# Three weight conversions shared with GpSimd and started a unit earlier, output rows in buffers of their own, and another end of the last block

## The chip, the cores and the metric

The kernel runs on one core of a Trainium2 chip. The core has five engines that run side by side and each take their own instructions strictly in order: PE (TensorE, matmuls and transposes), DVE (VectorE), ACT (ScalarE), POOL (GpSimd) and SP (SyncE, which here only issues DMAs). The metric is the device time of one execution in microseconds (us), the median of several runs.

## What is computed

The input is `q`, `k`, `v`, `alpha` of shape (4, 8, 768, 48) in float32 and two weight matrices in float64. A gated linear attention runs over the 768 positions, and its output goes through a feed-forward network (FFN) of 2048 hidden columns:

```python
for t in range(S):
    state = alpha[:, :, t, :, None] * state + np.einsum('bhd,bhe->bhde', k[:, :, t], v[:, :, t])
    y[:, :, t] = np.einsum('bhd,bhde->bhe', q[:, :, t], state)
x = np.ascontiguousarray(y.transpose(0, 2, 1, 3)).reshape(B * S, H * D)   # 3072 x 384
h = x @ w_in                                                              # 384 x 2048
g = np.maximum(0.01 * h, h)
out = g @ w_out                                                           # 2048 x 384
```

## The kernel before, in words

**Units and blocks.** The attention is cut into 24 units of 128 positions of one batch (4 batches at each of 6 places). Three units make a block of 384 rows, the FFN's moving size; there are 8 blocks. The FFN runs over 16 slices f of 128 hidden columns. `ffn_in(i, f)` is 9 matmuls (three groups of rows, each high*high, high*low and low*high part), then two passes on ACT and two on DVE that make `gh` and `gl`. `ffn_out(i, f)` is 9 matmuls into three PSUM banks, one for each unit of the block, summed over f. `finish(i)` copies the three banks out and stores them.

**The front.** Blocks 0 and 1 run interleaved over f, since the weights come in meanwhile: (0, f), (1, f). Before that, units 0 to 8 (`AHEAD` = 9) run through the attention alone; then PE has FFN work without a break. A unit's steps are: scans of alpha (`scans`, lines L283 to L298 with `pc`, `rc` on DVE and two small copies on POOL), `qs` and `ks` (L313, L321), scores on PE (L330), a copy on ACT and a triangular mask on POOL (L340, L341), the outputs `y` on PE (L368, L374), ACT's and DVE's halves of `y` into the tile `large` (L391, L392), and the new state (`us` L406 on DVE, a product on POOL L346). When a block's three units are done, `gather` sends two DMAs from `large` to `large` (L416); the FFN of that block waits for them.

**Conversions.** A slice's weights land in `raw` by five DMAs of SP: `w_out` (L192) and four pieces of `w_in` (L188), 786 KB together. `converting(f)` makes from each float64 a high and a low float32: on ACT a scaling of the top words (L224) and the rounded high part (L232); on DVE `bits` (L226, L229), the power `pw` (L236), the rest of the value (L238), the low words by their power (L240) and the sum (L243). The first three (f = 0, 1, 2, `EARLY`) run in the front, each placed behind the `ks` of unit 6, 7 and 8; the others run in the stage of blocks 0 and 1. The table `LOADS` says behind which DMA of the front the loads of the first four slices are issued.

**The order of the work.** The program is written step by step with generators; a scheduler then places each instruction on its engine, and `behind(key)` forbids it to place one ahead of a named instruction. What stands on an engine runs in that order whatever comes late. Buffers of a name (`t`, `o`, banks `a` and `b`) are handed out again when their last reader is done.

Of the kernel before, what the change touches and what calls it, by code (L numbers as in the profile page):

```python
# [9 lines left out]
F32 = mybir.dt.float32  # L10
# [12 lines left out]
def gated_linear_attn_ffn(ctx, tc, q, k, v, alpha, w_in, w_out, out):  # L23
    nc = tc.nc
# [180 lines left out]
    def converting(f, ordered=False):  # L205
# [31 lines left out]
        yield  # L237
        put(ordered, "DVE", lambda: nc.vector.tensor_tensor(val, val, hi.bitcast(F32), ALU.subtract))  # L238
# [5 lines left out]

    def convert(f):
        for _ in converting(f):
            pass
# [227 lines left out]
    pos = {}  # L475

    def ffn_out(i, f, gs, tag):
        gh, gl = gs
        if f == 0:
            pos[i] = [bank(tag)[:, 0:DM] for _ in range(UPB)]  # L480
        po = pos[i]
        for j in range(UPB):
            js = slice(j * C, (j + 1) * C)
            for n, (gt, wn) in enumerate(((gh, HIGH), (gh, LOW), (gl, HIGH))):
                nc.tensor.matmul(  # L485
                    po[j], gt[:, js], w_out_of(f, wn), start=f == 0 and n == 0, stop=f == NF - 1 and n == 2
                )
        if f == NF - 1:
            finish(i)

    def finish(i):
        for j, po in enumerate(pos.pop(i)):
            tb, b = units[i * UPB + j]
            o = ffp.tile([P, DM], F32, name="t")
            nc.scalar.copy(o, po)  # L495
            r = b * S + tb * C
            nc.sync.dma_start(out[r:r + P, :], o)
# [10 lines left out]
    LOADS = [(("v", 4), 0, 0), (("v", 5), 0, 1), (("v", 6), 1, 0), (("v", 7), 1, 1), (("g", 1), 2, None), (("g", 1), 3, None)]  # L508
# [3 lines left out]
    loaded_f = converted = 0  # L512
    for n, _ in enumerate(st):
        if n == 2:
            load_values(NV - 1)
        while LOADS and LOADS[0][0] in made:
            key, f, part = LOADS.pop(0)
            with behind(*key):
                load_weights(f, part)
            loaded_f = f + 1  # L520
        u = AHEAD - EARLY + converted
        if converted < EARLY and ("ks", u) in made:
            with behind("ks", u):
                convert(converted)
            converted += 1
        if n in STARTS:
            i, f = items[len(gs)][:2]
            with behind(*STARTS[n]):
                gs[len(gs)] = ffn_in(i, f)
# [175 lines left out]
```

## Time and profile before

| | |
|---|---|
| median of 3 runs | 541.69 us (540.21 to 541.97) |
| the profiled execution | 540.7 us |
| its span, first to last instruction | 539.0 us |
| PE busy | 520.6 us (97% of the span) |
| PE weight loads busy | 497.8 us (92%) |
| DVE busy | 380.3 us (71%) |
| ACT busy | 234.1 us (43%) |
| POOL busy | 64.5 us (12%) |
| granted TensorE clock, mean | 0.996 of full speed |

The share of an engine is a mean over stages that differ: the front (0 to about 71 us), blocks 0 and 1 (to about 167 us), and blocks 2 to 7 with the attention of units 9 to 23 between their matmuls. The profiled execution took 1.7 us more than its span, and 1.0 us less than the median of the runs.

### The profile page before, as it was taken

How to read it: one execution, taken by the hardware profiler on the slowest of the kernel's cores; microseconds unless marked ns; L12 is line 12 of the kernel's file. 1: busy time of each engine (PE TensorE's matmuls, PEld its weight loads, DVE VectorE, ACT ScalarE, POOL GpSimd, SP SyncE). 2: the span in 40 equal slices, each digit the busy share in tenths (PEclk: the TensorE clock that was granted, in tenths of full speed). 3: DMA queues.
4: the chain of work that ended last, by engine and by line, in shares of the span. 5: the costliest groups of instructions: out<-in, count | busy, mean ns of one | idle time of the engine just before them, and what ended most of it. 6: DMA issues, size and time to landing. Idle time of an engine off the chain costs nothing.

```text
span 539.0 us, 9954 instructions
## 1 busy us (share of the span) xinstructions
PE 520.6 (97%) x3742; PEld 497.8 (92%) x3742; DVE 380.3 (71%) x694; ACT 234.1 (43%) x494; POOL 64.5 (12%) x140
## 2 busy tenths in 40 slices
PE   6998899999999899999999999999999999999996
PEld 4787789999998799999999999999999999999995
DVE  6899999999999597875685775775876533333331
ACT  2675665545532543435334343344343344233332
POOL 4445420000000022110110101001100000000000
PEclk9998999999999999999999999999999999999999
DMA  9999954545825343433332422413301010101001
GB/s 146 164 177 184 202 140 131 142 111 134 190 43 144 114 107 85 102 79 103 71 82 58 105 64 61 105 42 99 69 1 40 0 45 1 23 0 45 0 1 49
DMA packets 92981, 46.62 MB, mean 86 GB/s; under 512 B 57856, under 2 KB 90112, under 8 KB 92928
## 3 DMA queue, kind: packets, MB, share of 16 engines
q1 hardware_dynamic: 92928, 45.93, 39.4%
q8 instruction: 31, 0.51, 0.4%
q14 instruction: 22, 0.18, 0.1%
HBM read 38.83 MB, written 4.72 MB: 81 GB/s over the span
## 4 chain that ended last, share of the span: by engine, by line
PE 87%; DVE 5%; DMA 3%; issue 1%; SPq 1%; POOL 1%; ACT 1%; DVEq 0%; ACTq 0%; POOLq 0%
PE ph L460 35%; PE b L485 32%; PE a L330 4%; PE a L485 4%; PE a L374 3%; PE a L368 2%; PE b L258 2%; PE a L353 1%; DMA raw<-in_moe_w_in_dram 1%; DMA out_dram<-t 1%; PE a L385 1%; DVE pc L288 1%; PE b L374 1%; PE a L258 1%; DVE rc L294 1%
## 5 line engine op out<-in xcount | busy, mean ns | idle before, releaser
L460 PE MATMUL ph<-large,w 128*128 128x384 f32 x1152 | 225.6, 338 | 3.1 <-DMA raw<-in_moe_w_in_dram 1.9
L460 PEld LDWEIGHTS ph<-large,w 128*128 128x128 f32 x1152 | 200.5, 188 | 5.4 <-DVE t L466 2.2
L485 PE MATMUL b<-w,gh 128*128 128x384 f32 x672 | 169.6, 340 | 1.3 <-ACT t L495 1.3
L466 DVE TENSOR_TENSOR t<-ph,t 128x384 f32<-128x384 f32 x128 | 70.3, 549 | 86.7 <-ACT t L463 86.3
L485 PEld LDWEIGHTS b<-w,gh 128*128 128x128 f32 x672 | 119.5, 188 | 3.7 <-ACT t L495 1.6
L463 ACT ACTIVATE t<-ph 128x384 f32<-128x384 f32 x128 | 62.6, 489 | 136.7 <-PE ph L460 128.6
L468 ACT CAST gh<-t 128x384 fp32r<-128x384 f32 x128 | 65.7, 513 | 108.2 <-DVE t L466 104.7
L485 PE MATMUL b<-w,gl 128*128 128x384 f32 x336 | 107.3, 336 | 0.0
L472 DVE TENSOR_TENSOR gl<-t,gh 128x384 fp32r<-128x384 f32 x128 | 70.3, 550 | 33.6 <-ACT gh L468 30.0
L485 PEld LDWEIGHTS b<-w,gl 128*128 128x128 f32 x336 | 62.6, 188 | 0.1
L341 POOL TENSOR_SCALAR_AFFINE_SELECT sm<-sm 128x512 f32<-128x512 f32 x33 | 21.9, 676 | 117.6 <-ACT sm L340 100.0
L346 POOL TENSOR_TENSOR small<-us,pe 48x192 f32<-48x192 f32 x40 | 25.5, 637 | 85.2 <-DVE us L406 75.3
L330 PEld LDWEIGHTS a<-qs,ks 48*128 48x128 f32 x312 | 26.0, 191 | 6.5 <-issue 5.2
L330 PE MATMUL a<-qs,ks 48*128 48x128 f32 x312 | 31.0, 289 | 0.9 <-DVE ks L321 0.9
L298 POOL COPY pe<-pc 128x4 f32<-128x4 f32 x24 | 5.7, 240 | 175.3 <-DVE pc L288 175.2
L262 DVE STREAM_TRANSPOSE ks<-small 128x512 f32<-128x512 f32 x15 | 16.6, 1119 | 13.6 <-PE a L353 13.6
L340 ACT COPY sm<-a 128x512 f32<-128x512 f32 x24 | 14.0, 584 | 15.1 <-PE b L330 13.3
L288 DVE TENSOR_TENSOR_SCAN pc<-e,small 128x128 f32<-128x128 f32 x60 | 19.9, 391 | 0.0
L485 PE MATMUL a<-w,gh 128*128 128x384 f32 x96 | 19.5, 335 | 0.0
L294 DVE TENSOR_TENSOR_SCAN rc<-e,small 128x511 f32<-128x511 f32 x15 | 19.1, 1272 | 0.2
L374 PE MATMUL a<-sm,small 128*48 128x128 f32 x256 | 18.1, 277 | 1.1 <-POOL sm L341 1.1
L224 ACT ACTIVATE raw<-raw 128x768 f32<-128x768 f32 x16 | 14.6, 915 | 7.0 <-DMA raw<-in_moe_w_in_dram 7.0
(82 smaller groups left out, 542.5 us busy)
## 6 DMA issues: line engine op xcount, KB each, us to landing
raw<-in_moe_w_out_dram SPq DMA_DIRECT2D x16, 384.0 KB, 4.0
small<-in_v_dram SPq DMA_DIRECT2D x24, 192.0 KB, 3.9
raw<-in_moe_w_in_dram SPq DMA_DIRECT2D x32, 144.0 KB, 4.0
out_dram<-t SPq DMA_DIRECT2D x24, 192.0 KB, 2.0
small<-in_alpha_dram SPq DMA_DIRECT2D x32, 96.0 KB, 2.2
small<-in_q_dram SPq DMA_DIRECT2D x30, 96.0 KB, 2.5
small<-in_k_dram SPq DMA_DIRECT2D x30, 96.0 KB, 2.2
small<-in_alpha_dram SPq DMA_DIRECT2D x30, 80.0 KB, 2.4
```

The lines of the kernel that those rows point to most:

```text
L288: nc.vector.tensor_tensor_scan(pc[:, p, :], aT[:, p, :], ones.broadcast_to([P, C]), 1.0, ALU.mult, ALU.mult)
L294: nc.vector.tensor_tensor_scan(flat[2][:, NP * C - 2::-1], flat[0][:, NP * C - 1:0:-1], flat[1][:, NP * C - 2::-1], last, ALU.mult, ALU.add)
L330: nc.tensor.matmul(ss[s][:, p, :], ks[lo:lo + D, p, :], qs[lo:lo + D, p, :], start=True, stop=True)
L341: nc.gpsimd.affine_select(out=sm[s], in_=sm[s], compare_op=ALU.is_ge, fill=0.0, base=0, pattern=[[0, NP], [1, C]], channel_multiplier=-1)
L346: nc.gpsimd.tensor_tensor(*scalings.pop(0))
L374: nc.tensor.matmul(y[lo:lo + m, p, :], V[:, c:c + m], masked[u][s][:, p, :], start=not tb and p == 0, stop=p == NP - 1, skip_group_check=True,
L460: nc.tensor.matmul(ph, w_in_of(f, wn, g), xt[:, g, :], start=n == 0, stop=n == 3 * NG - 1)
L463: put(ordered, "ACT", lambda: nc.scalar.mul(t, ph, 0.01))
L466: put(ordered, "DVE", lambda: nc.vector.tensor_tensor(t, ph, t, ALU.max))
L468: put(ordered, "ACT", lambda: nc.scalar.copy(gh, t))
L472: made["gl", i, f] = put(ordered, "DVE", lambda: nc.vector.tensor_tensor(gl, t, gh.bitcast(F32), ALU.subtract))
L485: nc.tensor.matmul(po[j], gt[:, js], w_out_of(f, wn), start=f == 0 and n == 0, stop=f == NF - 1 and n == 2)
```

## The change

Four things change. `converting` has a second form (`aside`) for f = 0, 1, 2: the low words are scaled by a second pass on ACT (L239 of the changed kernel), and the last three steps run on POOL, each in two halves of 384 columns (L242, L244, L246), put into the program one after the other while the units go on. These conversions stand behind the `ks` of units 5, 6 and 7, a unit earlier, and `LOADS` asks for the weights of f = 0, 1, 2 a unit earlier. The output rows have a name of their own, `o`, where they were `t`. For the last block, `ffn_out` keeps slice 14 back and issues 14 and 15 together bank by bank, and `finish` copies the three banks on ACT, DVE and both.

```diff
--- before.py
+++ after.py
@@ -202,7 +202,7 @@
             line.append(op(*args))
         return line[-1]
 
-    def converting(f, ordered=False):
+    def converting(f, ordered=False, aside=False):
 
         if f >= NF:
             return
@@ -235,16 +235,23 @@
         rest = pw.bitcast(F32)
         put(ordered, "DVE", lambda: nc.vector.tensor_scalar(pw, bits, -0x800000, None, ALU.bitwise_and))
         yield
+        if aside:
+            nc.scalar.mul(low.bitcast(F32), low.bitcast(U32), 2.0 ** -52)
+            yield
+            for half in (slice(0, DM), slice(DM, 2 * DM)):
+                nc.gpsimd.tensor_tensor(rest[:, half], rest[:, half], low[:, half].bitcast(F32), ALU.mult)
+                yield
+                nc.gpsimd.tensor_tensor(val[:, half], val[:, half], hi[:, half].bitcast(F32), ALU.subtract)
+                yield
+                made["w", f] = nc.gpsimd.tensor_tensor(lo[:, half], rest[:, half], val[:, half], ALU.add)
+                yield
+            return
         put(ordered, "DVE", lambda: nc.vector.tensor_tensor(val, val, hi.bitcast(F32), ALU.subtract))
         yield
         put(ordered, "DVE", lambda: nc.vector.scalar_tensor_tensor(
             rest, low.bitcast(U32), 2.0 ** -52, rest, ALU.mult, ALU.mult))
         yield
         made["w", f] = put(ordered, "DVE", lambda: nc.vector.tensor_tensor(lo, rest, val, ALU.add))
-
-    def convert(f):
-        for _ in converting(f):
-            pass
 
     def banks4():
         return bank().rearrange("r (p n) -> r p n", p=NP)
@@ -472,29 +479,42 @@
         made["gl", i, f] = put(ordered, "DVE", lambda: nc.vector.tensor_tensor(gl, t, gh.bitcast(F32), ALU.subtract))
         return gh, gl
 
-    pos = {}
+    pos, last = {}, []
 
     def ffn_out(i, f, gs, tag):
-        gh, gl = gs
         if f == 0:
             pos[i] = [bank(tag)[:, 0:DM] for _ in range(UPB)]
         po = pos[i]
+        last.append((f, gs))
+        if i == NB - 1 and f == NF - 2:
+            return
         for j in range(UPB):
             js = slice(j * C, (j + 1) * C)
-            for n, (gt, wn) in enumerate(((gh, HIGH), (gh, LOW), (gl, HIGH))):
-                nc.tensor.matmul(
-                    po[j], gt[:, js], w_out_of(f, wn), start=f == 0 and n == 0, stop=f == NF - 1 and n == 2
-                )
+            for f, (gh, gl) in last:
+                for n, (gt, wn) in enumerate(((gh, HIGH), (gh, LOW), (gl, HIGH))):
+                    nc.tensor.matmul(
+                        po[j], gt[:, js], w_out_of(f, wn), start=f == 0 and n == 0, stop=f == NF - 1 and n == 2
+                    )
+        last.clear()
         if f == NF - 1:
             finish(i)
 
     def finish(i):
         for j, po in enumerate(pos.pop(i)):
             tb, b = units[i * UPB + j]
-            o = ffp.tile([P, DM], F32, name="t")
-            nc.scalar.copy(o, po)
+            o = ffp.tile([P, DM], F32, name="o")
             r = b * S + tb * C
-            nc.sync.dma_start(out[r:r + P, :], o)
+            if i < NB - 1 or j == 0:
+                nc.scalar.copy(o, po)
+                nc.sync.dma_start(out[r:r + P, :], o)
+                continue
+
+            parts = [(nc.sync, nc.vector.tensor_copy, slice(0, DM))]
+            if j == UPB - 1:
+                parts = [(nc.sync, nc.vector.tensor_copy, slice(0, DM // 2)), (nc.scalar, nc.scalar.copy, slice(DM // 2, DM))]
+            for queue, copy, cs in parts:
+                copy(o[:, cs], po[:, cs])
+                queue.dma_start(out[r:r + P, cs], o[:, cs])
 
 
     items = []
@@ -505,11 +525,12 @@
-    LOADS = [(("v", 4), 0, 0), (("v", 5), 0, 1), (("v", 6), 1, 0), (("v", 7), 1, 1), (("g", 1), 2, None), (("g", 1), 3, None)]
+    LOADS = [(("v", 3), 0, 0), (("v", 4), 0, 1), (("v", 5), 1, 0), (("v", 6), 1, 1), (("v", 7), 2, None), (("g", 1), 3, None)]
 
     STARTS = {62: ("kt", 7), 65: ("kv", 7)}
     st = attention(0, AHEAD)
     loaded_f = converted = 0
+    early = []
     for n, _ in enumerate(st):
         if n == 2:
             load_values(NV - 1)
@@ -518,11 +539,17 @@
             with behind(*key):
                 load_weights(f, part)
             loaded_f = f + 1
-        u = AHEAD - EARLY + converted
+        u = AHEAD - 1 - EARLY + converted
         if converted < EARLY and ("ks", u) in made:
+            conv = converting(converted, aside=f64)
             with behind("ks", u):
-                convert(converted)
+                for _ in range(7):
+                    next(conv, None)
+            early.append(conv)
             converted += 1
+        for conv in early:
+            if next(conv, early) is not early:
+                break
         if n in STARTS:
             i, f = items[len(gs)][:2]
             with behind(*STARTS[n]):
```

What the scheduler makes of it is shown at three places. The first is SP near the end of the front. `raw_486` of before is slice 1, `raw_686` slice 2, `raw_692` slice 3; the three `small` rows are `q`, `k`, `v` of unit 8, and `large` is the gather of block 1. Before:

```order
L188 DMA raw_486<-in_moe_w_in_dram 48x3x128 x2
L188 DMA raw_486<-in_moe_w_in_dram 16x3x128 x2
L128 DMA small_73<-in_q_dram 128x8x48
L128 DMA small_73<-in_k_dram 128x8x48
L147 DMA small_73<-in_v_dram 128x8x48
L416 DMA large_74<-large_74 16x3x768
L192 DMA raw_686<-in_moe_w_out_dram 128x384
L188 DMA raw_686<-in_moe_w_in_dram 48x3x128 x2
L188 DMA raw_686<-in_moe_w_in_dram 16x3x128 x2
L416 DMA large_74<-large_74 16x3x768
```

In the changed program `raw_592` is slice 2 and `raw_708` slice 3; the first row is `v` of unit 7.

```order
L147 DMA small_73<-in_v_dram 128x8x48
L192 DMA raw_592<-in_moe_w_out_dram 128x384
L188 DMA raw_592<-in_moe_w_in_dram 48x3x128 x2
L188 DMA raw_592<-in_moe_w_in_dram 16x3x128 x2
L128 DMA small_73<-in_k_dram 128x8x48
L128 DMA small_73<-in_q_dram 128x8x48
L147 DMA small_73<-in_v_dram 128x8x48
L423 DMA large_74<-large_74 16x3x768 x2
L192 DMA raw_708<-in_moe_w_out_dram 128x384
L188 DMA raw_708<-in_moe_w_in_dram 48x3x128 x2
L188 DMA raw_708<-in_moe_w_in_dram 16x3x128 x2
```

The five loads of slice 2 have moved ahead of unit 8's loads, and both gathers now stand together, ahead of all of slice 3.

The second place is DVE and ACT around the conversion of slice 2. On DVE before, `bits_757` is slice 1, `bits_870` slice 2; `ks_867` and `qs_860` are unit 8's.

```order
L240 SCALAR_TENSOR_TENSOR pw_762<-raw_486,pw_762 128x768
L321 TENSOR_TENSOR ks_867<-a_862,rc_800 128x512
L313 TENSOR_TENSOR qs_860<-b_855,pc_799 128x512
L238 TENSOR_TENSOR bits_757<-bits_757,w1_756 128x768
L226 TENSOR_SCALAR bits_870<-raw_686 128x768
L466 TENSOR_TENSOR t_848<-ph_838,t_848 128x384
L406 TENSOR_TENSOR us_921<-small_73,a_893 48x192
L243 TENSOR_TENSOR w1_756<-pw_762,bits_757 128x768
L406 TENSOR_TENSOR us_921<-small_73,a_893 48x192
L392 TENSOR_TENSOR large_74<-b_880,large_74 112x4x128
L229 SCALAR_TENSOR_TENSOR bits_870<-raw_686,bits_870 128x768
```

On DVE now, `bits_776` is slice 2, `ks_773` and `qs_766` are unit 7's, `pc_820` unit 8's scan, and `large_74<-b_677` is unit 5's output, the last of block 1.

```order
L328 TENSOR_TENSOR ks_773<-a_768,rc_721 128x512
L226 TENSOR_SCALAR bits_776<-raw_592 128x768
L320 TENSOR_TENSOR qs_766<-b_761,pc_720 128x512
L229 SCALAR_TENSOR_TENSOR bits_776<-raw_592,bits_776 128x768
L413 TENSOR_TENSOR us_811<-small_73,a_799 48x192 x2
L399 TENSOR_TENSOR large_74<-b_677,large_74 112x4x128
L295 SCALAR_TENSOR_TENSOR pc_820<-b_815,small_73 128x128 x4
L236 TENSOR_SCALAR pw_781<-bits_776 128x768
L296 MEMSET b_815 128x32
L297 RECIPROCAL small_73<-pc_820 128x32
L301 SCALAR_TENSOR_TENSOR rc_821<-b_815,small_73 128x511
```

The first step of slice 2 stood behind unit 8's `ks` and `qs`, and stands now behind unit 7's `ks`, ahead of unit 7's `qs`, of unit 5's output and of all of unit 8. On ACT now, at the same place, the two passes over `raw_592` come first, then a score of unit 6 (`sm_745`) and unit 5's output.

```order
L239 ACTIVATE raw_592<-raw_592 128x768
L224 ACTIVATE raw_592<-raw_592 128x768
L347 COPY sm_745<-b_734 128x512
L398 CAST large_74<-b_677 112x4x128
L232 CAST w2_775<-bits_776 128x768
```

In the program of before the pass over slice 2's `raw` was followed by the FFN's `t` (L463), and unit 5's output was long made.

The third place is PE's last rows in the last block (`b_5443` to `b_5445` before and `b_5455` to `b_5457` now are the three banks, `w14`, `w15` the slices). Before:

```order
L485 MATMUL b_5445<-w14_1723,gh_5728 128x384 x2
L485 MATMUL b_5445<-w14_1723,gl_5730 128x384
L485 MATMUL b_5443<-w15_1786,gh_5754 128x384 x2
L485 MATMUL b_5444<-w15_1786,gh_5754 128x384 x2
L485 MATMUL b_5445<-w15_1786,gh_5754 128x384 x2
L485 MATMUL b_5443<-w15_1786,gl_5756 128x384
L485 MATMUL b_5444<-w15_1786,gl_5756 128x384
L485 MATMUL b_5445<-w15_1786,gl_5756 128x384
```

Now:

```order
L495 MATMUL b_5457<-w14_1735,gh_5740 128x384 x2
L495 MATMUL b_5457<-w14_1735,gl_5742 128x384
L495 MATMUL b_5455<-w15_1798,gh_5766 128x384 x2
L495 MATMUL b_5456<-w15_1798,gh_5766 128x384 x2
L495 MATMUL b_5457<-w15_1798,gh_5766 128x384 x2
L495 MATMUL b_5455<-w15_1798,gl_5768 128x384
L495 MATMUL b_5456<-w15_1798,gl_5768 128x384
L495 MATMUL b_5457<-w15_1798,gl_5768 128x384
```

The rows are the same but for numbers: the scheduler ends the banks with the last three matmuls, as before.

## Rows read from the trace of the kernel before

**Rows 1.** Windows of the trace: busy us and (instructions) per engine, clock, DMA share, GB/s.
```profile
40.00:60.00 20.00, 18.04 (x188) 15.34 (x189) 19.71 (x38) 11.12 (x26) 9.89 (x16) 0.91 1.13 193
60.00:80.00 20.00, 16.99 (x147) 16.03 (x143) 19.21 (x32) 11.90 (x24) 6.93 (x6) 1.00 0.68 163
80.00:160.00 80.00, 80.00 (x462) 80.00 (x461) 78.67 (x126) 42.07 (x74) 0.00 (x0) 1.00 0.51 124
160.00:180.00 20.00, 17.48 (x96) 16.21 (x95) 17.74 (x34) 6.10 (x14) 1.19 (x4) 1.00 0.57 144
```

**Rows 2.** Chain that ended last, 40 to 75 us: start, length, what.
```profile
55.39 6.42 DMA raw<-in_moe_w_in_dram
...
61.91 0.90 ACT raw L224
...
65.50 2.29 POOL small L346
...
67.85 2.30 POOL sm L341 x2
...
71.36 1.76 PE ph L460 x9
```

**Rows 3.** Timeline of SP's DMA issues, 46 to 56 us: start, length, what.
```profile
46.04 2.84 SPq L188 DMA_DIRECT2D raw<-in_moe_w_in_dram  x4
...
52.29 0.82 SPq L416 DMA_DIRECT2D large<-large  x1
53.16 0.57 SPq L192 DMA_DIRECT2D raw<-in_moe_w_out_dram  x1
53.79 2.19 SPq L188 DMA_DIRECT2D raw<-in_moe_w_in_dram  x4
56.03 0.59 SPq L416 DMA_DIRECT2D large<-large  x1
```

**Rows 4.** Tile raw, whole run: ns min/median/max per line; DMA issue to landing.
```profile
L224 ACT ACTIVATE raw<-raw x16: 888/915/938, 36.8 to 144.5; 128x768 f32<-128x768 f32 x16
...
DMA to landing us min/median/max: 2.9/3.9/7.4
```

**Rows 5.** VectorE lines by form, 40 to 75 us: busy us, mean ns, idle before.
```profile
L229 DVE SCALAR_TENSOR_TENSOR bits<-raw,bits 128x768 int32<-128x768 int32 x4 | 3.8, 940 | 0.0
L238 DVE TENSOR_TENSOR bits<-bits,w 128x768 f32<-128x768 f32 x3 | 3.6, 1193 | 0.0
L240 DVE SCALAR_TENSOR_TENSOR pw<-raw,pw 128x768 f32<-128x768 uint32 x3 | 3.1, 1030 | 0.0
...
L243 DVE TENSOR_TENSOR w<-pw,bits 128x768 fp32r<-128x768 f32 x3 | 2.8, 949 | 0.0
L406 DVE TENSOR_TENSOR us<-small,a 48x192 f32<-48x192 f32 x8 | 2.8, 345 | 0.1
L392 DVE TENSOR_TENSOR large<-b,large 112x512 fp32r<-112x512 f32 x4 | 2.7, 684 | 0.1
L226 DVE TENSOR_SCALAR bits<-raw 128x768 int32<-128x768 int32 x4 | 2.4, 596 | 0.6 <-ACT raw L224 0.6
```

**Rows 6.** One line of GpSimd each, whole run: ns min/median/max.
```profile
L346 POOL TENSOR_TENSOR small<-us,pe x40: 500/506/2282, 17.3 to 387.1; 48x192 f32<-48x192 f32 x40
...
L341 POOL TENSOR_SCALAR_AFFINE_SELECT sm<-sm x33: 630/634/1347, 12.6 to 450.9; 128x512 f32<-128x512 f32 x33
```

**Rows 7.** PE timeline in the change of blocks: start, length, what, idle before.
```profile
176.62 0.62 PE L485 MATMUL b<-w,gh 128*128 128x384 f32 x2 [1.26 <-ACT t L495]
...
179.73 1.83 PE L460 MATMUL ph<-large,w 128*128 128x384 f32 x9 [0.56 <-DVE t L466]
```

**Rows 8.** ScalarE timeline in the change of blocks.
```profile
176.08 0.86 ACT L495 COPY t<-b 128x384 f32<-128x384 f32 x2 [2.36 <-DMA out_dram<-t]
```

**Rows 9.** ScalarE timeline at the end.
```profile
533.40 1.24 ACT L495 COPY t<-b 128x384 f32<-128x384 f32 x3 [2.65 <-PE b L485]
```

**Rows 10.** SP timeline at the end.
```profile
533.90 1.74 SPq L497 DMA_DIRECT2D out_dram<-t  x3
```

## The prediction

> **What bounds the kernel now.** I read the windows first, to see which engine is full in which stage [rows 1]. From 80 to 160 us PE is busy 80.00 of 80 us with 462 instructions, so an FFN matmul takes 80 / 462 = 0.1732 us and nothing but fewer matmuls or an earlier start can shorten that stage. From 40 to 80 us PE has 5 us of gaps: VectorE is busy 19.71 and 19.21 of 20 us, and the DMA share is 1.13 in the first of these windows. From 160 to 180 us PE lacks 20 - 17.48 = 2.52 us. These two places, and the last microseconds, are all the change can touch.
>
> The chain of waits then says what the front's end hangs on [rows 2]: the last load of slice 2, issued at 55.39, takes 6.42 us to land; ACT's L224 follows at 61.91; then come POOL's product and masks, the last ending at 67.85 + 2.30 = 70.15, which is unit 8's; PE's first FFN group after it starts at 71.36. From there PE never waits. Blocks 0 and 1 have 2 x 16 x 18 = 576 matmuls; 27 were done by 70.15, and 71.36 + 549 x 0.1732 = 166.4 us is where blocks 0 and 1 end. So I need T, the end of unit 8's mask in the changed kernel: before it is 70.15.
>
> **The front: removed and moved.** On SP, the last loads of slice 1's `w_in` are issued until 46.04 + 2.84 = 48.88; then stood q, k, v of unit 8 and a gather until 53.16, and then slice 2's five loads, 0.57 + 2.19 us, with gaps 2.82, until 55.98 [rows 3]. Now the five loads stand directly behind unit 7's `v`, that is at 48.88 if nothing ahead of them moves (I keep that point: other loads move up too, but the queues are full there). They end at 51.70, the last one issued 0.59 us before that, at 51.1. Their landing I bound by the minimum and the worst near row, 2.9 and 6.42 us, with 3.9 the median [rows 2, 4]: 54.0, 55.0 or 57.5. I take 55.5, a little over the median, as the queues carry the same bytes as before. The price of the move is that unit 8's q, k, v are issued 2.8 us later; unit 8's scans wait for them, but DVE stands at slice 2 in that time, so I cost it at nothing; without that cover it would be up to 2.8 us.
>
> On ACT two passes over slice 2's `raw` now stand together; the new one (L239) I price like the old, 0.915 us [rows 4], bounds 0.888 and 0.938: 55.5 + 1.83 = 57.3. On DVE the first step of slice 2 waits for this and everything of units 7, 5 and 8 stands behind it. Before, DVE waited at this place for 0.6 us in all [rows 5]; now DVE, which sheds 9 instructions, 3 x (1.193 + 1.030 + 0.949) = 9.5 us [rows 5], reaches it early and spends the gain in waiting. From 57.3: L226 0.60, `qs` (as long as L392) 0.68, L229 0.94, two `us` 0.69, unit 5's output 0.68 [rows 5], together 3.6: 60.9 us. Unit 5's output is what block 1's gather waits for, and both gathers now stand on SP ahead of all of slice 3: 0.82 + 0.59 [rows 3] gives 62.3; slice 3's loads 2.82 gives 65.1; slice 4's 2.82 gives 67.9, the last one issued at 67.3. Landing at the median, 3.9 [rows 4]: 71.2. On ACT the pass over slice 4 stands ahead of unit 8's score copies: 0.915, and two copies of 512 columns at 1.24 / 3 x 512 / 384 = 0.55 each by ACT's copies of 384 [rows 9]: 73.2. Mask 0.63 [rows 6]: **T = 73.9**.
>
> What PE has done by then: 36 matmuls of `ffn_in` and 6 of `ffn_out` stand ahead of that mask in the changed program, 42 for 27, so 534 remain. T + 1.2 (as 71.36 - 70.15) + 534 x 0.1732 = T + 93.7 = 167.6, for 166.4 before: **+1.2 us**. Break-even is T = 72.7. The margin is thin, and the sum says that the earlier request for slice 2 buys nothing, because the wait for it has moved from ACT's last step to the middle of DVE's and SP's rows.
>
> **POOL's halves.** 3 x 6 instructions of 128x384 on two inputs. The trace has no such row. The nearest is POOL's product 48x192, 0.506 us at the median and 2.28 at worst [rows 6]. Twice 0.506 (twice the columns) is 1.01; the mask of 512 columns with one input takes 0.63, which gives a low end of 0.47 for 384. I take 0.95, nearer the upper one, as it too has two inputs: 17 us in all. POOL is busy 9.89 + 6.93 = 16.8 us of these 40 in 22 instructions [rows 1], so there is room for it: 40 + 17 + 16.8 = 73.8, just at T. I cost it at nothing; what hides it is POOL's idle 23 us. Without the stretched rows of POOL (22 x 0.506 = 11.1 us) the cover is 5.7 us wide, and with them it is gone.
>
> **Output rows in `o`.** In the change of blocks ACT's copies into `t` waited 2.36 us for an output DMA to release the buffer [rows 8], and PE waited 1.26 us for these copies and 0.56 for a `t` behind them [rows 7]. With a name of their own the copies wait for no output of the block just before. I take both, **-1.8 us**; bounds are 0 (PE's place is then held by DVE, which is busy 17.74 of 20 us [rows 1]) and all 2.5 that PE lacks there. In later blocks PE is full and there is nothing to win.
>
> **The last block.** In the program PE's last rows are the same as before: the banks still end with the last three matmuls, so "bank by bank" does not happen. What is left is the copies: 1.24 us for three in a row on ACT [rows 9], the DMAs issued in 1.74 us as they come [rows 10]. With DVE beside ACT, the last half ends perhaps one copy (0.41) earlier, less the wait of ACT's half for DVE's half: **-0.3 us**, bounds -0.8 (two copies of three hidden) and +0.2 (half a copy of wait more). The last half's DMA now starts from ACT's queue. The Trainium skill, "DMA: Bandwidth & Descriptors", section "Issuing engines are not separate DMA queues", says that issuing from another engine saves only the time on the issuing sequencer; by it, an estimate, one issue (1.74 / 3 = 0.6 us) is all there is to win here, and no row so far shows a DMA issued from ACT.
>
> **Sum.** 540.7 (profiled) + 1.2 - 1.8 - 0.3 = 539.8. The median of the runs stands 1.0 above the profiled execution: **540.8 us**. A difference under 0.3%, 1.6 us, is not told from no change by a measurement of this kernel.
>
> **Rivals.**
>
> *B: the front ends earlier.* If slices 2 and 4 land at the minimum, 2.9 us, T falls by 1.5 and 1.0 to 71.4: front -1.3. For it: the DMA share is 0.68 in the second window [rows 1], so slice 4 meets emptier queues, and loads in front of slice 2 have moved up. Against: 1.13 in the window in which slice 2 is asked for. 540.7 - 1.3 - 1.8 - 0.3 + 1.0 = 538.3; with the upper bounds of the other terms 537.1.
>
> *C: slices 2 and 4 land late (slower).* Both at 6.42, as slice 2's last load did [rows 2]: +2.0 and +2.5, T = 78.4, front +5.7, 545.3 us. This decides from T = 72.7 + 2.1 + 1.6 = 76.4 on, 2.5 us of landing more than I take. For it: the same saturated queues, and unit 7's and 8's loads in them. Against: it takes two bad landings.
>
> *D: POOL becomes the bound (slower).* POOL's product took 2.28 us where the median is 0.506, and two masks took 2.30 us [rows 2, 6] while VectorE ran operations on two SBUF inputs; of those, L238 has a mean of 1.193 in these rows [rows 5] for L243's 0.949 on the same shape. If a half takes 1.3 us, POOL ends at 40 + 23.4 + 16.8 = 80.2, T + 93.7 = 173.9, front +7.5, 547.1 us. It takes over from my T of 73.9 from 0.95 us per half on if the stretched rows stay, and from 1.27 if they go. Against: DVE sheds 9.5 us of just these two-input operations. The Trainium skill, "SBUF — State Buffer", section "Terms", states that DVE and GpSimd share a port pair that is locked for a whole instruction, and that the loser blocks; the trace agrees, with 2.28 for 0.506, and by that rule every half can block DVE as well as be blocked, which speaks against moving the work here and for this rival.
>
> **How the numbers follow.** Forecast 0.48, with its own range 539.0 to 542.2 (landing 1 us either way, `o` and end by their bounds); inside it lies mostly no change (0.34), some faster (0.14). B 0.26, all faster. C 0.15 and D 0.11, slower. So faster 0.40, within 0.3% 0.34, slower 0.26. The range goes from 536.8 (B with the upper bounds) to 545.4 (C), leaving out D and the ends of B and C.
>
> **What would show it.** Right: the last load of slice 2 issued near 51 and landed near 55.5; L226 of slice 2 waiting for ACT some 3 us or more, and DVE's busy share falling in 40 to 60; both gathers near 61 to 62; unit 8's mask ending near 74; PE's gaps in the change of blocks gone but for about 0.7 us; halves of 0.8 to 1.1 us on POOL. Wrong: slice 2's five loads issued well before 48.9 (B); a landing over 6 us (C); halves over 1.3 us, or the chain of waits running along POOL from 60 us on (D); PE still waiting for `t` after block 1 (the bound 0 of `o`).

## The result, and the profile after

The changed kernel takes 542.69 us (median of 20 runs, 540.42 to 545.90), the kernel before 540.73 us beside it (20 runs, 539.29 to 542.04): a ratio of 1.0039, interval 1.0023 to 1.0055, so 2 us slower. I had forecast 540.8 against 541.69, a little faster. The profiled execution took 542.21 us, its span is 540.5.

Three marks that both profiled executions have part the time: PE's first group of block 2 behind its 0.61 us wait for `t` (the end of blocks 0 and 1), the first output DMA of block 2, and the end.

| mark, us | before | after | difference |
|---|---|---|---|
| block 2's group behind the 0.61 us wait | 167.61 | 172.95 | +5.34 |
| block 2's first output DMA | 244.49 | 245.02 | +0.53 |
| end of the span | 539.0 | 540.5 | +1.5 |

So the front lost 5.3 us, the change of blocks and what follows it gave 4.8 back, and the rest lost 1.0 (0.4 of it the new end, below). The windows of after, columns as in [rows 1]:

```profile
40.00:60.00 20.00, 15.26 (x127) 12.69 (x126) 13.96 (x27) 11.33 (x24) 17.99 (x23) 0.81 0.95 153
60.00:80.00 20.00, 20.00 (x162) 17.34 (x162) 15.02 (x28) 12.56 (x28) 11.35 (x17) 0.93 0.75 173
80.00:160.00 80.00, 80.00 (x478) 79.95 (x474) 75.67 (x122) 41.17 (x73) 2.19 (x2) 1.00 0.50 128
160.00:180.00 20.00, 19.39 (x111) 19.07 (x111) 19.77 (x38) 7.55 (x18) 1.20 (x4) 1.00 0.40 108
```

From 40 to 60 us PE fell from 18.04 to 15.26 us and its clock from 0.91 to 0.81. VectorE, full before, fell from 19.71 to 13.96: the work taken off it left only waiting. GpSimd rose from 9.89 to 17.99 of 20 us. From 60 us on PE has no gap. The front's loss in this pair of traces is not idle time of PE: up to the first mark it issues the same 1192 instructions in both traces, idle for 10.6 us before and 10.9 now, but busy for 156.4 us before and 161.5 now. From 40 to 72 us it is busy as long as before and gets through fewer instructions (PE alone: us, busy, clock, DMA share, GB/s; first before, then after):

```profile
40.00:72.00 32.00, 27.03 (x284) 0.95 1.03 198
40.00:72.00 32.00, 27.25 (x221) 0.84 0.94 177
```

Two things make PE's work longer there. It stands at 1.2 GHz for 10.2 us, where it was 3.4 before (added up from windows of 2 us). At that clock a group of nine FFN matmuls takes 3.15 us, at 2.4 GHz 1.72 to 1.86, so these 6.8 us more cost up to 3.4 (an estimate). And unit 7's scores, which before the change took 1.1 us in one row, now stand apart and take twice that:

```profile
57.70 1.16 PE L337 MATMUL a<-qs,ks 48*128 48x128 f32 x8
...
63.47 1.16 PE L337 MATMUL b<-qs,ks 48*128 48x128 f32 x8
```

The chain of waits from 52 to 57 us runs along GpSimd:

```profile
52.12 1.02 POOL pw L242
53.14 0.96 POOL bits L244
54.10 0.98 POOL pw L242
55.07 0.97 POOL bits L244
56.04 0.60 POOL sm L348
...
56.69 0.42 PE b L381 x2
```

Four halves in a row, 0.96 to 1.02 us each, then a mask, then PE, which had waited 1.0 us for it. That is PE's only wait for a mask from 36 to 82 us; before the change there were two, 1.1 us together (with the same conversions and the old end, a run below, there are two of 3.0 together). So what late masks do to PE shows less in its waits than in the order and the clock of its work. Start, length and idle time on GpSimd a little later, and at unit 8's two masks:

```profile
55.99 0.64 POOL L348 TENSOR_SCALAR_AFFINE_SELECT sm<-sm 128x512 f32<-128x512 f32 x1
56.59 2.99 POOL L246 TENSOR_TENSOR w<-pw,bits 128x384 fp32r<-128x384 f32 x2
59.54 0.64 POOL L348 TENSOR_SCALAR_AFFINE_SELECT sm<-sm 128x512 f32<-128x512 f32 x1
...
74.69 1.23 POOL L348 TENSOR_SCALAR_AFFINE_SELECT sm<-sm 128x512 f32<-128x512 f32 x2 [4.35 <-ACT sm L347]
```

And ScalarE's copies that feed these masks:

```profile
51.11 0.58 ACT L347 COPY sm<-a 128x512 f32<-128x512 f32 x1
...
54.39 0.92 ACT L239 ACTIVATE raw<-raw 128x768 f32<-128x768 uint32 x1 [0.84 <-DMA raw<-in_moe_w_in_dram]
55.21 0.89 ACT L224 ACTIVATE raw<-raw 128x768 f32<-128x768 f32 x1
55.99 0.57 ACT L347 COPY sm<-b 128x512 f32<-128x512 f32 x1
```

The copy L347 of 51.11 ended at 51.69, its mask started at 55.99: 4.3 us behind four halves. The copy of 55.99 ended at 56.56, its mask started at 59.54: 3.0 us behind two halves, which took 2.99. On VectorE, slice 2's first step and unit 5's output:

```profile
56.12 0.92 DVE L226 TENSOR_SCALAR bits<-raw 128x768 int32<-128x768 int32 x1 [2.79 <-ACT raw L224]
...
59.40 0.69 DVE L399 TENSOR_TENSOR large<-b,large 112x512 fp32r<-112x512 f32 x1
```

SP's issues of slice 2, of the two gathers, and of slices 3 and 4 (for [rows 3]):

```profile
47.49 1.14 SPq L192 DMA_DIRECT2D raw<-in_moe_w_out_dram  x1
48.68 2.47 SPq L188 DMA_DIRECT2D raw<-in_moe_w_in_dram  x4
...
60.12 1.22 SPq L423 DMA_DIRECT2D large<-large  x2
61.43 0.53 SPq L192 DMA_DIRECT2D raw<-in_moe_w_out_dram  x1
...
64.93 2.19 SPq L188 DMA_DIRECT2D raw<-in_moe_w_in_dram  x4
```

In the change of blocks PE's waits of 1.26 and 0.56 us [rows 7] are gone; the 0.61 us ahead of block 2 stays:

```profile
172.95 1.83 PE L467 MATMUL ph<-large,w 128*128 128x384 f32 x9 [0.61 <-DVE t L473]
...
179.31 1.72 PE L467 MATMUL ph<-large,w 128*128 128x384 f32 x9
```

The last output DMAs (KB each, median us from issue to landing): the half rows take 3.4 and 3.6 us where whole rows take 2.8. But three whole rows at the end take 2.8 in the trace before and 3.4 in the traces with o and the old end, so that the size delays them is not shown.

```profile
out_dram<-o SPq DMA_DIRECT2D x2, 192.0 KB, 2.8
out_dram<-o ACTq DMA_DIRECT2D x1, 96.0 KB, 3.4
out_dram<-o SPq DMA_DIRECT2D x1, 96.0 KB, 3.6
```

### The profile page after: what moved, and what is told of

Same layout as the page of the kernel before. It is cut to its first block, busy times and chain, and to the rows that moved or that the text cites. A ratio compares the mean times of both kernels' runs of the same rounds, so it can differ in the third digit from the quotient of the medians.

```text
span 540.5 us, 9951 instructions
## 1 busy us (share of the span) xinstructions
PE 522.6 (97%) x3742; PEld 500.2 (93%) x3742; DVE 374.6 (69%) x687; ACT 234.9 (43%) x496; POOL 78.4 (15%) x158
## 4 chain that ended last, share of the span: by engine, by line
PE 89%; DVE 4%; DMA 3%; issue 1%; POOL 1%; SPq 0%; DVEq 0%; ACT 0%
PE ph L467 37%; PE b L495 33%; PE a L495 4%; PE a L337 4%; PE a L381 3%; PE a L375 3%; DMA small<-in_q_dram 2%; PE b L265 2%; DVE pc L295 1%; PE a L360 1%; DVE rc L301 1%; PE a L392 1%; DMA raw<-in_moe_w_out_dram 1%; PE b L381 1%; PE a L265 1%
## 5 line engine op out<-in xcount | busy, mean ns | idle before, releaser
L353 POOL TENSOR_TENSOR small<-us,pe 48x192 f32<-48x192 f32 x40 | 22.5, 563 | 79.3 <-DVE us L413 74.0
L347 ACT COPY sm<-a 128x512 f32<-128x512 f32 x24 | 14.0, 585 | 12.9 <-PE b L337 11.0
L232 ACT CAST w<-bits 128x768 fp32r<-128x768 f32 x16 | 13.4, 836 | 10.9 <-DVE bits L229 10.9
```

The lines of the kernel that those rows point to most:

```text
L353: nc.gpsimd.tensor_tensor(*scalings.pop(0))
```

## The experiments

All times beside the kernel before on the same chip; "ratio" is to that, so runs of different groups compare by it. It is not the quotient of the medians and differs from it by up to 0.0015. 0.001 is 0.54 us. "Early" is the changed kernel's loads and places, "old" those of before; o is in all but the second, and the end is that of before except where the new one is named.

| conversions of the front | masks of units 5 to 8 | median us | ratio, interval |
|---|---|---|---|
| old, VectorE (o alone) | GpSimd | 535.49 | 0.9916, 0.9901 to 0.9931 |
| changed, rows still `t` | GpSimd | 544.22 | 1.0084, 1.0058 to 1.0111 |
| changed (early, ScalarE's pass, halves) | GpSimd | 542.56 | 1.0047, 1.0029 to 1.0064 |
| early, VectorE, new end | GpSimd | 538.47 | 0.9963, 0.9949 to 0.9977 |
| old, ScalarE's pass, halves | GpSimd | 542.72 | 1.0036, 1.0021 to 1.0050 |
| old, VectorE; scores not in turns | GpSimd | 546.33 | 1.0105, 1.0071 to 1.0139 |
| old, VectorE, new end | GpSimd | 535.78 | 0.9917, 0.9895 to 0.9940 |
| old, one step in halves | GpSimd | 535.74 | 0.9905, 0.9882 to 0.9927 |
| old, VectorE; 18 idle halves | GpSimd | 543.22 | 1.0038, 1.0020 to 1.0056 |
| old, ScalarE's pass, steps on VectorE | GpSimd | 539.88 | 0.9980, 0.9966 to 0.9995 |
| old, VectorE's pass, halves | GpSimd | 539.64 | 0.9975, 0.9959 to 0.9990 |
| early, VectorE's pass, halves | GpSimd | 542.62 | 1.0021, 1.0002 to 1.0039 |
| changed, halves behind a unit's masks | GpSimd | 539.61 | 0.9962, 0.9938 to 0.9986 |
| old, VectorE's pass, halves | VectorE | 535.44 | 0.9882, 0.9847 to 0.9918 |
| early, ScalarE's pass, steps on VectorE | GpSimd | 536.65 | 0.9904, 0.9872 to 0.9935 |
| old, VectorE | VectorE | 538.91 | 0.9953, 0.9934 to 0.9973 |
| changed | VectorE | 537.69 | 0.9942, 0.9926 to 0.9958 |

**o alone.** The kernel before with one name changed:

```diff
-            o = ffp.tile([P, DM], F32, name="t")
+            o = ffp.tile([P, DM], F32, name="o")
```

> The kernel before with output rows named o, and nothing else. Theory 1 (of my three terms only o gains): PE loses its 1.3 and 0.6 us waits in the change of blocks, so 1.5 to 2.5 us under before, some 538.7 us. Theory 2 (the wait for t is only moved to VectorE, busy there): within 0.5 us of before.

It gains 5.0 us, twice the most that either theory allowed. Block 2's first output DMA stands 71.65 us behind the first mark, 76.88 before: 5.2 us. PE's named waits, 1.8 us, are the smaller part. Another is in work that PE is busy with: the scores of two units. One of them before (PE, start and length):

```profile
181.49 1.16 PE L330 MATMUL a<-qs,ks 48*128 48x128 f32 x8
...
184.34 1.16 PE L330 MATMUL a<-qs,ks 48*128 48x128 f32 x8
```

With o alone:

```profile
175.68 1.16 PE L330 MATMUL a<-qs,ks 48*128 48x128 f32 x16
```

The same 16 matmuls of a unit stand in one row and take 1.16 us, where two rows of 8, each one half of the rows, took 1.16 each. The other unit's 16 take 1.70 us with o alone, for 2 x 1.16. From 160 to 250 us the score matmuls take 8.11 us before and 6.35 with o alone. That these rows stood apart I put down to the order that the scheduler found with copies that wait; no run tried it. L374 and L385 beside them lost 0.8 us in the same way (7.26 to 6.43 us from 166.8 to 250). Some 0.8 us of the 5.2 I cannot place.

**Scores not in turns.** The two loops exchanged, on o alone:

```diff
-        for p in range(NP):
-            for s, lo in ((0, 0), (1, HB)):
+        for s, lo in ((0, 0), (1, HB)):
+            for p in range(NP):
```

> o alone, and the scores of a unit written one half of the rows after the other instead of in turns. Theory 1 (score matmuls of rows 0 to 47 and of rows 64 to 111 overlap on PE when they stand in turns, and what o gained beyond PE's named waits came from two units whose halves no longer stand apart): 0.9 to 1.2 us for each of the 15 units from block 2 on, 13 to 18 us more, 549 to 553 us. Theory 2 (their order makes no difference, the gain came from elsewhere): within 2 us of 535.5.

0.0189 over o alone, 10 us: the order matters. A unit's 16 now take 1.71 us:

```profile
265.32 1.71 PE L330 MATMUL a<-qs,ks 48*128 48x128 f32 x16
```

That is 0.55 us each for the 15 units from block 2 on, 8.3 us, less than I expected: side by side they still overlap in part, and only halves that stand apart cost the whole 1.16. Of the rest, some stands in the front, whose scores are exchanged too: the first mark is at 169.68 for 166.78. The time is that of two executions. The Trainium skill, "TensorE: Matmul & The Clock Gate", section "Part 3: Packing small matmuls — row/col tiling", says that matmuls on different row groups run at the same time; the runs agree, with 1.16 us for 16 in turns and for 8 of one half.

**The conversions alone, and the end of before.** The first takes the changed kernel with `ffn_out` and `finish` of before, the second the same with rows in o.

> The changed conversions and loads alone; output rows are t and the last block ends as before. Theory 1 (the front got worse, by two more stretches of 3.4 us at PE's lower clock, each worth 1.7 us at most): 2 to 4 us over before, some 543.7 us, and a mean granted clock under 0.993. Theory 2 (the front is even, the loss of the whole change sits in its end): within 1 us of before.

> The changed kernel with the last block's end of before (three copies on ScalarE, three whole rows stored by SP), o kept. Theory 1 (the half rows land 0.8 us later, so the new end loses): 0.7 to 1.3 us faster than the changed kernel, some 541.6 us, 0.9 over before. Theory 2 (the end gains, as I forecast, 0.3 us): 0.3 us slower than the changed kernel, 543.0 us.

The conversions alone lose 3.7 us by the medians, 4.5 by the ratio; the loss is in the front (the first mark is at 172.43 for 167.61), not in the end. The clock too is as theory 1 of that run had it: 0.988 to 0.992 in its executions, under 0.993. With the conversions in place o gains only 1.7 us (544.22 to 542.56), so the terms do not simply add. Without the new end the changed kernel takes 542.56 us against 542.69: the medians can't tell the ends apart.

**The new end on o alone.**

> o and the new end of the last block, conversions as before. Theory 1 (half rows land later, so the new end costs 0.4 to 0.9 us from block 2's outputs to the end): 536.1 us, and in the trace the last output DMA lands 3.4 us or more after its issue. Theory 2 (it gains 0.3 us as I forecast): 535.2 us, landing 2.8 us.

0.3 us more by the medians, inside the intervals. In the profiled executions the way from block 2's first output DMA to the end is 295.29 us with the new end and 294.97 with the old; in the changed kernel 295.48 and 295.04. The half rows land in 3.2 and 3.4 us here, the whole rows of the run with o alone in 3.4. So the new end gains nothing, and costs 0.3 to 0.4 us in these pairs of traces.

**Early, all on VectorE.**

```diff
-            conv = converting(converted, aside=f64)
+            conv = converting(converted)
```

> The changed kernel, but the early conversions keep their last three steps on VectorE at full width; loads and place stay a unit earlier. Theory 1 (the early loads and the order they force make the front worse, and GpSimd helps): VectorE has 9.5 us more to do, 2 us or more over the changed kernel, some 545 us. Theory 2 (GpSimd's halves are what costs, as they hold masks and products up and stretch VectorE's operations): 2 us or more under the changed kernel, some 540.5 us.

0.0084 under the changed kernel with the old end (0.0076 under the changed kernel itself), some 4 us, although VectorE does all. The edit takes away GpSimd's halves and ScalarE's second pass together, so one or both of them cost, and theory 1 of this run falls. The places of before (and `LOADS` of before), with the halves:

```diff
-        u = AHEAD - 1 - EARLY + converted
+        u = AHEAD - EARLY + converted
```

> The conversions of the front with their last three steps on GpSimd in halves, but loads and places as before the change; rows in o, the last block ends as before. Beside the run with o alone (0.9916 of before, 535.5 us). Theory 1 (18 halves of 1 us hold up the masks and products that stand behind them on GpSimd, wherever they stand): 3 to 4 us more, some 539 us. Theory 2 (only the earlier loads and places together with GpSimd lose): at most 1 us more, 536.5 us.

0.0120 over o alone, 6.5 us, more than either theory: the halves with ScalarE's pass don't need the early loads to lose.

**Which part of the new conversion.** It moves three things: time on GpSimd, a second pass on ScalarE, and who waits for whom. Idle halves on GpSimd; ScalarE's pass without halves; halves without ScalarE's pass, at the old and at the early places (the second and third cut are against the changed conversions):

```diff
+            for _ in range(6):
+                nc.gpsimd.tensor_tensor(idle[0], idle[0], idle[1], ALU.mult)
```
```diff
-            for half in (slice(0, DM), slice(DM, 2 * DM)):
-                nc.gpsimd.tensor_tensor(rest[:, half], rest[:, half], low[:, half].bitcast(F32), ALU.mult)
...
+            nc.vector.tensor_tensor(rest, rest, low.bitcast(F32), ALU.mult)
+            nc.vector.tensor_tensor(val, val, hi.bitcast(F32), ALU.subtract)
+            made["w", f] = nc.vector.tensor_tensor(lo, rest, val, ALU.add)
```
```diff
-            nc.scalar.mul(low.bitcast(F32), low.bitcast(U32), 2.0 ** -52)
+            nc.vector.tensor_scalar(low.bitcast(F32), low.bitcast(U32), 2.0 ** -52, None, ALU.mult)
```

> o alone; the front's conversions stay on VectorE, and GpSimd gets 18 multiplications of 128x384 on two tiles that nobody else reads, at the places where its halves would be put. Theory P (GpSimd's time itself: masks and products wait behind the halves): 2 to 5 us over 535.5. Theory A (ScalarE's second pass over raw and what stands behind it) and theory D (others wait for the results of GpSimd's halves): within 1 us of 535.5.

> o alone, with ScalarE's second pass over raw (the scaling of the low words) and the last three steps on VectorE at full width; nothing of the conversion on GpSimd; places as before. Theory A: near the run with GpSimd's halves at the old places (542.7 us), 540 to 543. Theories P and D: within 1.5 us of 535.5.

> o alone, the scaling of the low words as a pass on VectorE instead of ScalarE, the halves on GpSimd, places as before. Theory A: 536 to 538 us (three passes of some 0.6 us more on VectorE). Theories P and D: 540 us or more, as with ScalarE's pass.

> The changed kernel's conversions and loads, a unit earlier, halves on GpSimd, o, the end as before, but the scaling of the low words as a pass on VectorE instead of ScalarE. Theory A: near the run with the early conversions on VectorE, 537 to 539.5 us. Theories P and D: 541 to 543.5 us, as the same kernel with ScalarE's pass (542.6).

No theory has all four, and only the last result lies in a stated range. The idle halves alone cost 0.0122 over o alone, 6.6 us: time on GpSimd is enough. But the scheduler put them earlier than I meant, all 18 before 37 us and 9 of them from 20 us on, many directly ahead of a mask, as here:

```profile
32.20 1.00 POOL L249 TENSOR_TENSOR idle<-idle,idle 128x384 f32<-128x384 f32 x1
33.15 0.64 POOL L351 TENSOR_SCALAR_AFFINE_SELECT sm<-sm 128x512 f32<-128x512 f32 x1
```

so this run shows that time on GpSimd can cost that much, not that it does at the real places. ScalarE's pass without halves costs 3.5 us at the old places (two of VectorE's steps are put in a little later there as well). There (ScalarE's waits, 36 to 82 us: total, times, longest) it stands for 6.4 us waiting for a slice to land, with a unit's copies behind it:

```profile
ACT raw L239 <- DMA raw<-in_moe_w_in_dram: 10.0, 2, 6.4
```

The halves without that pass cost 3.2 us at the old places. At the early places the exchange of ScalarE's pass for one on VectorE saves 1.4 us by the ratios (1.0047 to 1.0021, the intervals overlap) and nothing by the medians, and 5.7 us over o alone stay: theory A falls for the changed kernel.

**One step of the three in halves.** The subtraction alone on GpSimd, 6 halves:

```diff
-        put(ordered, "DVE", lambda: nc.vector.tensor_tensor(val, val, hi.bitcast(F32), ALU.subtract))
+        if ordered:
+            put(ordered, "DVE", lambda: nc.vector.tensor_tensor(val, val, hi.bitcast(F32), ALU.subtract))
+        else:
+            for half in (slice(0, DM), slice(DM, 2 * DM)):
+                nc.gpsimd.tensor_tensor(val[:, half], val[:, half], hi[:, half].bitcast(F32), ALU.subtract)
```

> o alone, and of the front's conversions only the subtraction (L238) on GpSimd in two halves, 6 halves in all, places as before. Theory 1 (any half on GpSimd holds a mask or a product up by its 1 us): 1 to 2 us over 535.5. Theory 2 (VectorE, full in the front, is relieved of 3.6 us, and 6 halves fit GpSimd's idle time): 1 to 2 us under it.

No difference from o alone, so neither theory held. That a third of the halves finds room on GpSimd would fit; what VectorE's relief gives back was not measured apart.

**The masks.** GpSimd runs a unit's masks and products in one row with the halves. The changed conversions with each slice's halves kept behind a unit's masks; and the masks of units 5 to 8 on VectorE:

```diff
-                for _ in range(7):
+                for _ in range(6):
...
+            with behind("mask", u):
+                if next(conv, early) is not early:
```
```diff
-            if s and u >= AHEAD:
+            if s and u >= AHEAD or 5 <= u < AHEAD:
                 nc.vector.tensor_tensor(sm[s], ss[s], mask.unsqueeze(1).broadcast_to([P, NP, C]), ALU.mult)
```

> The changed conversions and loads, o, the end as before, and each slice's halves placed behind the masks of the unit behind whose ks the slice stands. Theory M (the halves cost because a unit's masks wait behind them): 2 us or more under the same kernel without this (542.6 at 1.0047 of before), a ratio of 1.001 or less. Theory R (GpSimd is full here in any order, or others wait for its results): within 1 us of it, 1.003 to 1.007.

> o, the scaling of the low words as a pass on VectorE, the halves on GpSimd, places as before, and the masks of units 5 to 8 as one multiplication on VectorE straight from PSUM (it replaces ScalarE's copy and GpSimd's mask). Beside the same masks without the halves. Theory M: within 1.5 us of that run. Theory R: 3 us or more over it.

> o alone and the masks of units 5 to 8 on VectorE straight from PSUM; conversions as before. VectorE is full there and gets 8 x 0.68 = 5.4 us more, ScalarE loses 8 copies: 2 to 5 us over 535.5 if VectorE's order decides the front, at most 1 us over if the masks were the wait that ends last.

> o, loads and places a unit earlier, ScalarE's second pass over raw, the last three steps on VectorE at full width, the end as before. If the costs of the halves and of ScalarE's pass simply add at these places too: 1.5 us over the early run with all on VectorE (538.5 at 0.9963 of before), 0.998 to 1.001 of before. If the pass costs 3.5 us here as at the old places: 1.002 to 1.004.

> The changed conversions and loads (a unit earlier, ScalarE's pass, halves on GpSimd), o, the end as before, and the masks of units 5 to 8 on VectorE straight from PSUM. Theory M: the whole loss of the halves comes back, 0.986 to 0.992 of before. Rival (the rest is GpSimd's products and small copies behind the halves): 0.995 to 1.000.

The order alone, with every half still there, gives back 0.0085, 4.6 us. On GpSimd both masks of a unit now run together, ahead of the next slice's halves:

```profile
53.03 1.22 POOL L348 TENSOR_SCALAR_AFFINE_SELECT sm<-sm 128x512 f32<-128x512 f32 x2
55.51 1.03 POOL L242 TENSOR_TENSOR pw<-pw,raw 128x384 f32<-128x384 f32 x1 [1.26 <-DVE pw L236]
```

With the masks off GpSimd the halves cost nothing: at the old places the run with halves is at 0.9882 and the one without at 0.9953, 3.8 us less, where the halves cost 3.2 with the masks beside them. The windows, 40 to 80 us, with halves:

```profile
40.00:60.00 20.00, 16.74 (x182) 14.62 (x180) 19.30 (x39) 7.85 (x18) 10.21 (x16) 0.91 1.16 201
60.00:80.00 20.00, 19.32 (x153) 17.05 (x152) 18.83 (x28) 10.80 (x21) 16.36 (x16) 1.00 0.57 153
```

and without:

```profile
40.00:60.00 20.00, 15.17 (x142) 12.60 (x141) 19.10 (x38) 6.10 (x12) 5.03 (x9) 0.77 1.13 197
60.00:80.00 20.00, 20.00 (x179) 19.11 (x178) 19.74 (x33) 12.47 (x26) 2.82 (x4) 0.97 0.53 139
```

GpSimd is full with the halves, 16.36 of 20 us, and PE waits for it once between 36 and 82 us, 0.6 us. Theory R falls; theory M's own range, within 1.5 us, is missed on the other side. That the halves themselves gain is not shown, since the clock parts the two runs (PE, with halves and without):

```profile
40.00:72.00 32.00, 28.18 (x291) 0.95 0.94 187
40.00:72.00 32.00, 27.17 (x250) 0.84 0.94 185
```

PE stands at 1.2 GHz for 3.4 us with the halves and for 10.3 without, and the mean clocks of the executions are 0.995 to 0.998 and 0.984 to 0.991. These 6.9 us cost up to 3.4 (an estimate as above), nearly the whole difference.

The fourth run tells what the early places and ScalarE's pass cost without halves: 0.9904, nothing over o alone, so neither of its two expectations held. By it the halves of the changed kernel cost 1.0047 - 0.9904 = 0.0143, 7.7 us, all of its front's loss. Part of that is the clock: the mean over the executions is 0.9897 with the halves and 0.9965 without, which on 540 us is up to 3.7 (an estimate). Behind the masks the halves still cost 0.9962 - 0.9904 = 0.0058, 3.1 us; why is open. With the masks on VectorE the changed kernel itself comes to 0.9942, 5.7 us back, between what I had expected of the theory and of its rival. 2 us stay, as much as these masks cost VectorE in the run without halves (0.9953 against 0.9916); that they are the same 2 us was not tried. In the trace of this run PE idles as long up to the first mark as in that of the changed kernel with the old end, 12.5 and 12.4 us; what came back is busy time, 160.3 to 154.9 us, and no stretch at 1.2 GHz is left for the 6.8 us there. Why one order of the front brings the clock down and another does not was not tried.

## Why the prediction was wrong

**The sum.** It was +1.2 (front), -1.8 (o), -0.3 (end). Measured one by one: front +7.1 us (1.0047 against 0.9916), o -5.0 us, end between 0 and +0.4. Two errors of 6 and 3 us with opposite signs left the change 3 us from the forecast one (+2.0 for -0.9), and on the other side of zero; that they come this near to cancelling is luck. The split hangs on the order: with the conversions taken first they lose 3.7 us, and o then gains 1.7, close to my 1.8. Two ranges of the prediction don't follow from their terms: the ends of the whole range, 536.8 and 545.4, stand for the rivals' own 537.1 and 545.3, and the forecast's own 539.0 to 542.2 would be 538.6 to 544.1 with all the bounds that it names.

**The step that failed** is "I cost it at nothing; what hides it is POOL's idle 23 us". The price of a half was right: 0.96 to 1.02 us alone for the 0.95 that I took, 1.02 to 1.18 on average of each kind. But the idle time of a window hides work only if nothing in the row behind is due: masks stood 4.3 and 3.0 us behind halves, and the order alone, halves behind the masks, gives 4.6 of the 7.7 us back. Little of it came as waiting: PE waited 1.0 us for masks in this trace (3.0 in the one with the old end) where it was 1.1 before, and was busy 5.1 us longer over the same 1192 instructions, at 1.2 GHz for 10.2 us instead of 3.4 and with unit 7's scores apart. My sum has no term for PE's own work getting longer. I worked out when GpSimd's row would end, 73.8, and not what waits in its middle. My rival D had this engine and this price, "from 0.95 us per half on if the stretched rows stay", and the wrong mechanism: it is not the sum that binds, as 16.36 of 20 us without masks cost nothing in that run.

**The chain of the front** came out nearly as told: slice 2 issued from 47.49 to 51.15 (I said 48.88 to 51.70), landed by 54.39 (55.5), VectorE's first step waited 2.79 us (3 or more) and ran at 56.12, unit 5's output ended at 60.09 (60.9), the gathers were issued by 61.34 (62.3), slice 4 by 67.12 (67.9). Unit 8's mask ended at 75.92 for 73.9. What failed is the formula behind it, T + 93.7, which gives 169.6: I took the 42 matmuls that stand ahead of the mask as done by then; about 34 were (27 and part of the nine from 74.52 on). PE had been late since 57 us and had not waited for that mask at all; it worked off its row without a gap until 172.3. What stands ahead in a row is not what is done.

**o** was the right mechanism, mis-sized: -1.8, with an upper bound of 2.5, for -5.0. The bound was PE's idle time; PE being busy 60 of 60 us from 180 to 240 hid a loss in the order of its matmuls.

**The end**: as told, PE's last rows did not change. The gain of 0.3 from copies side by side is not there: the ends differ by 0.3 to 0.4 us the other way.

**The rivals.** B's time did not come, though slice 2 landed a microsecond sooner than I took, most of the way to B's 54.0; nor did C's late landing. No rival had PE's clock.

The simplest of the best runs is the kernel before with o alone, 0.9916. The run with halves and the masks on VectorE (0.9882), the early one with ScalarE's pass (0.9904) and the one with a single step in halves (0.9905) have intervals that overlap it; which is best is open.

## What to carry to other kernels

Before work is moved onto an idle engine, list what stands behind each place in its row and when that is due; a few 1 us operations ahead of a short step on the way to PE cost 7.7 us net here, and 3.1 when they stood behind it. A buffer name shared between a copy that leaves by DMA and one that PE waits for is worth a look of its own: the wait that the profile names can be the smaller part, since a late copy also changes the order in which the work behind it is laid out. And an engine that is busy 100% can still hold time: compare how long the same instructions take in the two traces, and the clock of the same stretch, before a difference is put down to the edit itself.

## What the runs showed of the hardware

PE's matmuls on rows 0 to 47 and 64 to 111 overlap when they are issued in turns: 16 in 1.16 us, 1.71 when one half follows the other, 2 x 1.16 when they stand apart.

The granted clock fell three times in the front of the changed kernel and once before. PE was busy 0.46 of 2 us from 46 to 48, at 1.00; from 50 to 52 it was busy throughout at half, 1.2 GHz (windows; us, PE, PEld, DVE, ACT, POOL, clock, DMA share, GB/s):

```profile
46.00:48.00 2.00, 0.46 (x14) 0.21 (x8) 1.93 (x8) 0.92 (x2) 2.00 (x3) 1.00 1.24 196
...
50.00:52.00 2.00, 2.00 (x15) 1.78 (x13) 1.99 (x3) 1.53 (x3) 0.39 (x1) 0.50 0.98 299
...
60.00:62.00 2.00, 2.00 (x8) 2.00 (x7) 2.00 (x8) 1.74 (x6) 1.85 (x4) 0.50 0.28 66
```

The scores of unit 6 took 1.95 us there (48.81 to 50.76) for 1.16 at 2.4 GHz. Up to 3.4 of the front's 5.3 us runs through these stretches, by the estimate above; no run held the order of the work and changed the clock alone. Of the 20 runs the one with the highest mean clock, 0.995, was the fastest (540.42) and the one with the lowest, 0.985, the slowest (545.90).

A half on GpSimd took 1.00 us on average in the run with idle halves (20 to 80 us), 1.02 to 1.18 in the changed kernel by step, and 1.37 in the run with one step in halves.
